# Half of the first in-projection of token blocks 2 and 3 by seven block products for eight, with the units of the second MLP made later

## The chip, the cores and the metric

The kernel runs on one core of a Trainium2 chip. The metric is the device time of one execution in microseconds (us); three runs of the kernel before gave 1089.79, 1090.01 and 1091.31 us, and their median, 1090.01 us, is the time before. A profiled execution is one more run, with its own time. PE is TensorE, DVE is VectorE, ACT is ScalarE, POOL is GpSimd, and SP is the engine whose queue issues nearly all DMAs.

## What is computed

A retention layer (linear attention with a decay per head) is followed by two MLPs, all in float32, for 4 x 768 = 3072 tokens with 8 heads of 64 (so 512 features):

```python
state = gamma[None, :, None, None] * state + np.einsum('bhd,bhe->bhde', k[:, :, t], v[:, :, t])
y[:, :, t] = scale * np.einsum('bhd,bhde->bhe', q[:, :, t], state)
...
h = np.maximum(x @ w_in, 0.0)
x = h * h @ w_out
...
xn = x / rms * rms_g
g = xn @ w_gate
out = (g * (1.0 / (1.0 + np.exp(-g)))) * (xn @ w_val) @ w_out
```

`w_in` is 512 x 2048, `w_out` 2048 x 512; `w_gate` and `w_val` are 512 x 1536, and the second `w_out` 1536 x 512.

## The kernel before

**Arithmetic.** Every large product keeps float32 accuracy with a matmul type of fewer mantissa bits: an operand is split into a high and a low part (`split`, L99: an ACT copy to the high part, then a DVE subtraction, `low`, L96), and one product is three matmuls, high by high, high by low and low by high (`mm3`, L243; `proj`, L279). Weights come as 64-bit integers and are turned to float32 on the chip by a "tick" (L221): an ACT activation over the raw tile, two DVE instructions (L208, L209), then the split.

**Token blocks.** The tokens are six blocks of 512. The order of the program is written out by hand (`manual_schedule`), and each engine runs its instructions in that order.

1. Block 0, then block 1 (`block1`, L1139): for each of 16 column chunks f of `w_in`, 12 matmuls of the in-projection (`proj`), ReLU and square (`act1`), the split of the result s, and one chunk later 12 matmuls of the out-projection (`tail1`, `out1`). During block 0 the first MLP's weights are converted, two ticks a chunk.
2. Blocks 2 and 3 together: `in_phase` (L416) runs 16 chunks f times 2 blocks t, each 12 matmuls over the resident weights `W["i", f]`, into PSUM banks `ph`, with ReLU and square by ACT.
3. The out-projection of blocks 2 and 3, and everything of blocks 4 and 5 and of the second MLP, goes by Strassen's scheme: 7 products of half-size blocks for 8. A weight operand of such a product is a "unit" (512 KB: high and low part), stored in DRAM and read through a ring of seven SBUF tiles, one unit for each product of 12 matmuls. `in_pair` (L767) makes four chunks of `w_in` for two token blocks from 7 products P1, P2, P6, P5, P7, P3, P4; `pair` (L712) does the same for the second MLP.
4. The second MLP runs for s = 0, 1, 2 (two token blocks each): six `pair`s, then the out-projection. For s = 0 its weight units are made in the same pairs (`make_unit`, L670).

**Making units.** `made_units` (L143) makes four of the seven units (P5, P7, P6, P3) of a quarter q of a weight matrix in five steps, from two "rows" tiles that hold the quarter in float32: step 1 is two DVE adds or subtractions of 128x512, step 2 a split (P5), steps 3 and 4 a subtraction and a split each (P7, P6), step 5 a split (P3). The other three units (P1, P2, P4) are stored directly from the split weights (`keep_units`, L138; `keep_in`, L1228). For the first MLP the rows tiles are summed again from the split weights by four DVE adds a quarter (`whole_rows`, L1185), so a quarter takes seven steps. The out-weights' steps (`made`) are taken two a chunk in block 1, the in-weights' (`made_in`) one a chunk from f = 4 of block 1 on and then in `in_phase`, quarter order 0, 1, 2, 3. The units of the second MLP's out-weights (`makers`) are made in `in_phase`, from rows tiles that stay in SBUF from their ticks on. Those ticks begin in block 1 at chunk MORE_AT + 1 = 13.

**Retention.** The tokens come in 24 chunks of 128; chunks 8 to 15 are "visited" (`visit`, L974) in block 1 at even f, chunks 16 to 23 in `in_phase` at odd f. A visit is some 64 small matmuls through the banks `pr`, whose scores land in another bank and are masked by DVE (`mask`, L905, six instructions). `after_visit` (L983) copies the result out of `pr` (a split for blocks 2 and 3, a plain ACT copy for blocks 4 and 5), adds to the state on DVE, and issues the loads for two chunks on. POOL multiplies state, v and q by their decays (L959, L881, L870).

**Storage.** 38 SBUF tiles of 4 KB a partition serve weights, operands, ring, rows and raw loads alike; a new tile waits for the last use of the one whose place it takes. `stores()` issues the DMAs put off in `later`.

**Where order binds** (the program's order of DVE around the end of block 1):

```python
if f in visit_at:
    after_visit(at_chunk, sink(at_chunk), kv)
...
last_of(f)
tail1()
prev = (f, s, j)
```

`last_of` (here `last1`, L1254) holds `made`, the tick and `made_in`; `tail1` is the out-projection of the chunk before. The low part of s of chunk f therefore stands in DVE's queue behind all that `last1` of chunk f - 1 put there.

## Time and profile before

| | |
|---|---|
| median of three runs | 1090.01 us |
| profiled execution: its own time | 1091.34 us |
| its span, first to last instruction | 1089.6 us |
| PE busy | 1084.2 us, 6305 matmuls |
| DVE busy | 793.4 us, 1109 instructions |
| ACT busy | 565.9 us, 877 instructions |
| POOL busy | 74.9 us, 65 instructions |
| DMA | 277.79 MB, mean 255 GB/s |
| granted TensorE clock, mean | 0.999 |

The span is what the engines show; 1.7 us of the profiled time lie around it. Shares of busy time are averages over stages that differ: what an edit costs is read from the stage that it is in. A matmul's duration in the rows (0.39 us) is its way through the array; the pace at which they follow one another is the difference of their starts.

Stages in the trace, by the starts of PE's groups: block 0 until 117 us, block 1 from 117.5 to 229.5, `in_phase` from 229.5 to 341.3, the out-projection of blocks 2 and 3 to 417.7, `in_pair`s of blocks 4 and 5 to 494, their out-projection to 570.9, then the second MLP, whose six pairs of s = 0 run from 570.87 to 685.

### The profile page before, as it was taken

How to read it: one execution, taken by the hardware profiler on the slowest of the kernel's cores; microseconds unless marked ns; L12 is line 12 of the kernel's file. 1: busy time of each engine (PE TensorE's matmuls, PEld its weight loads, DVE VectorE, ACT ScalarE, POOL GpSimd, SP SyncE). 2: the span in 40 equal slices, each digit the busy share in tenths (PEclk: the TensorE clock that was granted, in tenths of full speed). 3: DMA queues.
4: the chain of work that ended last, by engine and by line, in shares of the span. 5: the costliest groups of instructions: out<-in, count | busy, mean ns of one | idle time of the engine just before them, and what ended most of it. 6: DMA issues, size and time to landing. Idle time of an engine off the chain costs nothing.

```text
span 1089.6 us, 16607 instructions
## 1 busy us (share of the span) xinstructions
PE 1084.2 (100%) x6305; PEld 893.1 (82%) x6305; DVE 793.4 (73%) x1109; ACT 565.9 (52%) x877; POOL 74.9 (7%) x65
## 2 busy tenths in 40 slices
PE   9999999999999999999999999999999999999998
PEld 7788888887888888888888888888888888888887
DVE  6988689989976996578887676995333896433585
ACT  5777434467767546785455555453332554233442
POOL 3000142214210000000000000000000000000000
PEclk9999999999999999999999999999999999999999
DMA  9964678898999669985646769667667567666563
GB/s 362 356 213 148 217 247 301 300 364 297 347 379 350 219 231 398 367 293 193 212 174 250 270 242 350 221 211 250 194 232 251 193 213 249 193 193 194 193 212 117
DMA packets 100963, 277.79 MB, mean 255 GB/s; under 512 B 10212, under 2 KB 33532, under 8 KB 100884
## 3 DMA queue, kind: packets, MB, share of 16 engines
q1 hardware_dynamic: 100704, 276.49, 72.7%
q8 instruction: 50, 0.82, 0.3%
q10 hardware_dynamic: 180, 0.24, 0.1%
q14 instruction: 29, 0.24, 0.1%
HBM read 195.41 MB, written 81.28 MB: 254 GB/s over the span
## 4 chain that ended last, share of the span: by engine, by line
PE 97%; DMA 1%; DVE 1%; ACT 0%; issue 0%; ACTq 0%; SPq 0%
PE ph L286 14%; PE ph L244 9%; PE ph L246 9%; PE ph L245 9%; PE pa L244 8%; PE pa L246 8%; PE pa L245 8%; PE pb L244 5%; PE pb L246 5%; PE pb L245 5%; PE pr L244 3%; PE pr L246 3%; PE pr L245 3%; PE pr L939 2%; PE pr L948 1%; PE pr L928 1%
## 5 line engine op out<-in xcount | busy, mean ns | idle before, releaser
L286 PE MATMUL ph<-xh,w_i 128*128 128x512 f32 x504 | 162.6, 392 | 0.1
L467 ACT CAST o<-act 128x1024 fp32r<-128x1024 f32 x101 | 105.6, 1052 | 109.4 <-DVE act L104 50.6
L97 DVE TENSOR_TENSOR o<-act,o 128x1024 fp32r<-128x1024 f32 x101 | 122.9, 1219 | 29.1 <-ACT o L467 29.0
L286 PEld LDWEIGHTS ph<-xh,w_i 128*128 128x128 f32 x504 | 94.5, 188 | 21.1 <-ACT act L426 0.5
L286 PE MATMUL ph<-xl,w_i 128*128 128x512 f32 x252 | 97.6, 389 | 0.0
L245 PE MATMUL ph<-o,ring 128*128 128x512 f32 x228 | 88.6, 389 | 0.0
L246 PE MATMUL ph<-o,ring 128*128 128x512 f32 x228 | 88.5, 388 | 0.0
L244 PE MATMUL ph<-o,ring 128*128 128x512 f32 x228 | 88.5, 388 | 0.0
L244 PE MATMUL ph<-xop,ring 128*128 128x512 f32 x176 | 68.6, 390 | 0.0
L245 PE MATMUL ph<-xop,ring 128*128 128x512 f32 x176 | 68.5, 389 | 0.0
L246 PE MATMUL ph<-xop,ring 128*128 128x512 f32 x176 | 68.5, 389 | 0.0
L244 PE MATMUL pa<-xop,ring 128*128 128x512 f32 x176 | 68.5, 389 | 0.0
L245 PE MATMUL pa<-xop,ring 128*128 128x512 f32 x176 | 68.5, 389 | 0.0
L246 PE MATMUL pa<-xop,ring 128*128 128x512 f32 x176 | 68.5, 389 | 0.0
L245 PE MATMUL pb<-xop,ring 128*128 128x512 f32 x176 | 68.5, 389 | 0.0
L244 PE MATMUL pb<-xop,ring 128*128 128x512 f32 x176 | 68.5, 389 | 0.0
L246 PE MATMUL pb<-xop,ring 128*128 128x512 f32 x176 | 68.5, 389 | 0.0
L107 DVE TENSOR_TENSOR part<-pr,part 128x512 f32<-128x512 f32 x38 | 25.9, 689 | 55.7 <-ACT part L111 54.4
L104 DVE TENSOR_TENSOR act<-act 128x1024 f32<-128x1024 f32 x52 | 63.4, 1219 | 0.3
L111 ACT COPY part<-ph 128x512 f32<-128x512 f32 x52 | 30.3, 587 | 58.6 <-PE ph L246 58.4
L706 ACT ACTIVATE t<-part 128x512 f32<-128x512 f32 x54 | 34.1, 632 | 46.8 <-DVE part L107 46.8
L286 PEld LDWEIGHTS ph<-xl,w_i 128*128 128x128 f32 x252 | 47.3, 188 | 9.5
(249 smaller groups left out, 2520.3 us busy)
## 6 DMA issues: line engine op xcount, KB each, us to landing
ring<-wu SPq DMA_DIRECT2D x84, 512.0 KB, 4.2
ring<-up SPq DMA_DIRECT2D x63, 512.0 KB, 4.3
ring<-uo SPq DMA_DIRECT2D x56, 512.0 KB, 4.1
wu<-ring SPq DMA_DIRECT2D x42, 512.0 KB, 5.5
ring<-ui SPq DMA_DIRECT2D x28, 512.0 KB, 5.2
raw<-w1i SPq DMA_DIRECT2D x16, 512.0 KB, 9.2
raw<-w1o SPq DMA_DIRECT2D x16, 512.0 KB, 8.7
vkt<-vk SPq DMA_DIRECT2D x16, 512.0 KB, 5.6
```

Source lines behind the costliest of these rows:

```text
L97: eng.tensor_tensor(out=dst_l, in0=src, in1=dst_h.bitcast(F32), op=ALU.subtract)
L104: eng.tensor_tensor(out=out_, in0=a, in1=b, op=ALU.subtract)
L107: eng.tensor_tensor(out=out_, in0=a, in1=b, op=ALU.add)
L111: nc.scalar.copy(dst[:, m], acc[m])
L244: nc.tensor.matmul(acc, ah, bh, start=start, stop=False, **more)
L245: nc.tensor.matmul(acc, ah, bl, start=False, stop=False, **more)
L246: nc.tensor.matmul(acc, al, bh, start=False, stop=stop, **more)
L286: nc.tensor.matmul(h, w[:, a, k * 128:(k + 1) * 128], x[b][k], start=n == 0, stop=n == len(order) - 1)
L467: nc.scalar.copy(h, src)
L706: nc.scalar.activation(t, g, AF.Silu)
L928: nc.tensor.matmul(kv[b, p, :], kk[:, p, h, :], vv[:, p, h, :], start=True, stop=True)
L939: nc.tensor.matmul(a[heads[h ^ SWAP[p]], :], vv[:, p, h, :], P[:, h, p, :], start=(p == 0 or two and p == 2), stop=(c < B and p in (1, 3)) ...
```

## The change

`in_phase` keeps chunks 0 to 7 only (NCL = 4 pairs of chunks). Chunks 8 to 15 are made by two `in_pair`s, n = 2 and 3, ahead of the out-projection. For that

- blocks 2 and 3 leave the visits of block 1 as plain copies (`Raw`), and a new generator, `first_x`, makes the operands P1 and P2 (block 2) at f = 10 and 12 of block 1, `other` and P3 (block 3) at f = 14, and the rest in the eight chunks of `in_phase`;
- float32 rows of the chunks 8 to 15 of both first-MLP weights are stored to DRAM (`kept`) when they are converted in block 0; `whole_rows` loads them back for quarters 2 and 3 in place of its DVE adds, so those quarters take six steps; the in-weights' quarters are made in the order 2, 3, 0, 1;
- visits 20 to 23, eight ticks and the last unit steps move into the two pairs (`after1b`); ticks begin at f = 10 of block 1 (MORE_AT = 9);
- the seven ring tiles are loaded at f = 1 to 7 of `in_phase`, first with in-units of quarters 2 and 3;
- the rows of the second MLP's out-weights go to DRAM (`rows2`), and `made_late` loads them and makes those units in the first pairs of s = 0: one step before `act2` of P1 (`first`), two after P6 (`second`), one after P3 (`third`).

```diff
@@ -39,13 +39,14 @@
-MORE_AT = 12
+MORE_AT = 9
-RING_AT = 12
+NCL = 4
+RING_AT = 16
...
+    rows2 = [[dram.tile([128, 2, 512], F32, name=f"rows_p{q}{r}") for r in range(2)] for q in range(NQ2)]
+    kept = {(k, n): dram.tile([128, 2, 512], F32, name=f"rows_{k}{n}") for k in "io" for n in range(NCL, 2 * NQ)}
...
@@ -126,9 +129,11 @@
         t = slot(f"w_{key[0]}{key[1]}", F32R)
         W[key] = t
         nc.scalar.copy(t[:, 0, :], f)
+        if key[1] >= 2 * NCL:
+            nc.sync.dma_start(kept[key[0], key[1] // 2][:, key[1] % 2, :], f)
         return lambda: low(eng or nc.vector, t[:, 1, :], f, t[:, 0, :])
...
-    def make_some():
-        if makers and next(makers[0], makers) is makers:
-            makers.pop(0)
+    def made_late():
+        for q in range(NQ2):
+            rows = [slot("rows") for _ in range(2)]
+            for to, kept_rows in zip(rows, rows2[q]):
+                nc.sync.dma_start(to, kept_rows)
+            yield
+            yield from made_units(uo2, q, rows, lambda: slot("sm")[:, 0, :])
 
             if n % 4 == 3:
-                makers.append(made_units(uo2, n // 4, row_tiles.pop(n // 4), lambda: slot("sm")[:, 0, :]))
+                for to, rows in zip(rows2[n // 4], row_tiles.pop(n // 4)):
+                    later.append(lambda to=to, rows=rows: nc.sync.dma_start(to, rows))
...
     def magnitude(i):
         if i < upto[0] and i not in sizes:
             key = steps[i][1]
-            sizes[i] = row_of(key[1]) if key[0] == "p" else cf.tile([128, 512], F32, tag="f", name="f")
+            if key[0] == "p":
+                sizes[i] = row_of(key[1])
+            elif key[0] in "io" and key[1] >= 2 * NCL and i % 3 == 0:
+                sizes[i] = tp.tile([128, TB], F32, tag="y", name="f")
+            else:
+                sizes[i] = cf.tile([128, 512], F32, tag="f", name="f")
...
     def in_phase(xs, w_of, after, between):
-        for f in range(NF1):
+        for f in range(2 * NCL):
...
+    def first_x(raws, xs):
+        y = {(h, t): raws[t].t[:, 2 * h:2 * h + 2, :] for h in range(2) for t in range(2)}
+
+        def put(src, wide=False):
+            if wide:
+                t = big("xop", F32R)
+                o = [t[:, 0:2], t[:, 2:4]]
+            else:
+                o = [slot("xop", F32R) for _ in range(2)]
+            split(*o, src, nc.vector)
+            return o
+
+        yield
+        X[P1] = put(y[0, 0])
+        yield
+        X[P2] = put(y[1, 0])
+        yield
+        other = put(y[0, 1])
+        X[P3] = put(y[1, 1])
+        for a in ((X[P1], X[P2]), (other, X[P3])):
+            xs.append([[a[k // 2][n][:, k % 2, :] for k in range(KC)] for n in range(2)])
+        yield
+        sub(y[0, 0], y[0, 1], y[0, 0])
+        yield
+        X[P5] = put(y[0, 0])
+        yield
+        sub(y[0, 1], y[1, 1], y[0, 1])
+        yield
+        X[P7] = put(y[0, 1], True)
+        yield
+        sub(y[1, 1], y[1, 1], y[0, 0])
+        yield
+        X[P6] = put(y[1, 1])
+        yield
+        sub(y[1, 0], y[1, 0], y[1, 1])
+        yield
+        X[P4] = put(y[1, 0], True)
         yield
...
             rows = row_tiles[key, q] = [slot("rows") for _ in range(2)]
+            if 2 * q >= NCL:
+                for r in range(2):
+                    nc.sync.dma_start(rows[r], kept[key, 2 * q + r])
+                yield
+                return
...
         def in_units():
-            for q in range(NQ):
+            for q in (2, 3, 0, 1):
...
         def sink1(c):
+            nonlocal coming_xs
             t = c // B - 2
-            if t == len(xs):
-                xs.append(Operand(t == 0))
-            return xs[t]
+            if t == len(raws1):
+                raws1.append(Raw())
+                if t:
+                    coming_xs = first_x(raws1, xs)
+                    next(coming_xs)
+            return raws1[t]
...
+        def more_ring():
+            n = len(ring)
+            ring.append(slot(f"ring{n}", F32R))
+            nc.sync.dma_start(ring[n].bitcast(F32), stream[n])
+
+        stream += [ui[q][k] for q in range(NCL // 2, NQ) for k in IN_ORDER]
         def last1(f):
             stores()
+            if f >= RING_AT:
+                more_ring()
             if f == MORE_AT:
                 more_steps(W2_SOON)
@@ -1260,6 +1333,8 @@
                 tick()
             if f >= 4:
                 next(made_in, None)
+            if f in (10, 12, 14):
+                next(coming_xs)
...
+        def next_chunk():
+            nonlocal at_chunk
+            decay_v(at_chunk + 1, nc.gpsimd)
+            decay_q(at_chunk + 2, nc.gpsimd)
+            at_chunk += 1
+
         def after1(f, t):
-            nonlocal at_chunk
             if t == 0:
                 stores()
                 tick(ahead=f < 8)
                 if f and f % 2 == 0:
-                    decay_v(at_chunk + 1, nc.gpsimd)
-                    decay_q(at_chunk + 2, nc.gpsimd)
-                    at_chunk += 1
-            elif f in (10, 12, 14):
-                tick(ahead=False)
+                    next_chunk()
             elif f % 2:
                 kv, _ = visit(at_chunk, pa, True)
                 after_visit(at_chunk, sink2(at_chunk), kv)
-            if t or f not in (2, 4, 6, 8):
-                make_some()
+            if t:
+                next(coming_xs, None)
             if f % 2 == 0 or t == 0:
                 next(made_in, None)
-            if f >= RING_AT and t:
+            if t and f and len(ring) < 7:
                 more_ring()
-            if (f, t) in ((14, 1), (15, 0), (15, 1)):
-                n = (f - 14) * 2 + t - 1
-                out_1.hi(n)
-                out_1.lo(n)
-
-        def more_ring():
-            n = len(ring)
-            ring.append(slot(f"ring{n}", F32R))
-            nc.sync.dma_start(ring[n].bitcast(F32), stream[n])
+
+        def after1b(n, k):
+            background()
+            mask()
+            stores()
+            if k in (P1, P5, P7, P4):
+                tick(ahead=False)
+            if (n, k) == (NCL // 2, P1) or k == P5 or k == P4 and n < NQ - 1:
+                next_chunk()
+            if k in (P6, P3):
+                kv, _ = visit(at_chunk, (ph, pb)[(n + 1) % 2] if k == P6 else pa, True)
+                after_visit(at_chunk, sink2(at_chunk), kv)
+            if k in (P1, P5, P7, P4):
+                next(made_in, None)
+            if n == NQ - 1 and k in (P2, P6, P3):
+                i = (P2, P6, P3).index(k)
+                out_1.hi(i)
+                out_1.lo(i)
 
         in_phase(xs, lambda f: W[("i", f)], after1, between1)
-        while len(ring) < 7:
-            more_ring()
+        for _ in coming_xs:
+            pass
+        for n in range(NCL // 2, NQ):
+            in_pair(n, after1b)
+        for a in last_square:
+            square_of(a)
+        last_square.clear()
         while back:
             if due:
                 sums(pa[0])
             background()
 
-        while makers:
-            make_some()
         for _ in made_in:
             pass
         stores()
...
+                def make_late(n):
+                    for _ in range(n if s == 0 else 0):
+                        next(making, None)
+
                 def first():
+                    make_late(1)
...
                 def second():
                     nonlocal coming
+                    make_late(2)
...
                 def third():
+                    make_late(1)
```

## Rows read from the trace of the kernel before

**Rows 1.** The page: busy time by engine; the chain that ended last, by engine.

```profile
PE 1084.2 (100%) x6305; PEld 893.1 (82%) x6305; DVE 793.4 (73%) x1109; ACT 565.9 (52%) x877; POOL 74.9 (7%) x65
...
PE 97%; DMA 1%; DVE 1%; ACT 0%; issue 0%; ACTq 0%; SPq 0%
```

**Rows 2.** Windows: length, busy PE, PEld, DVE, ACT, POOL; clock, DMA share, GB/s.

```profile
20.00:33.00 13.00, 12.88 (x95) 9.51 (x93) 11.71 (x21) 10.44 (x19) 2.97 (x2) 1.00 1.03 405
...
180.00:229.50 49.50, 49.37 (x419) 40.55 (x418) 48.04 (x83) 25.29 (x47) 15.82 (x12) 1.00 0.87 313
229.50:341.30 111.80, 111.70 (x949) 91.22 (x947) 91.83 (x161) 76.32 (x137) 24.87 (x20) 1.00 0.94 341
...
608.95:627.99 19.04, 19.04 (x86) 15.77 (x85) 13.74 (x21) 9.44 (x17) 0.00 (x0) 1.00 0.64 234
```

**Rows 3.** Chain in order of time, PE, start of in_phase: start, length, what.

```profile
235.09 8.16 PE ph L286 x36
```

**Rows 4.** Timeline of DVE, end of block 1: start, length, instruction, [idle before, releaser].

```profile
193.58 0.42 DVE L911 TENSOR_TENSOR causal<-ph,seen_sb 128x256 f32<-128x256 f32 x1 [0.76 <-PE ph L893]
...
195.49 0.69 DVE L97 TENSOR_TENSOR s<-r,s 128x512 fp32r<-128x512 f32 x1
...
198.84 3.24 DVE L107 TENSOR_TENSOR rows<-w_o 128x512 f32<-128x512 f32 x2
...
202.87 1.22 DVE L107 TENSOR_TENSOR rows<-w_o 128x512 f32<-128x512 f32 x2
...
212.22 2.55 DVE L107 TENSOR_TENSOR rows<-w_i 128x512 f32<-128x512 f32 x2
...
224.41 0.75 DVE L97 TENSOR_TENSOR xl<-pr,xh 128x256 fp32r<-128x256 f32 x2
...
229.92 0.68 DVE L97 TENSOR_TENSOR s<-r,s 128x512 fp32r<-128x512 f32 x1
```

**Rows 5.** Timeline of POOL, after a visit of block 1.

```profile
198.34 1.49 POOL L881 TENSOR_TENSOR vkt<-vkt,vdec_sb 128x512 f32<-128x512 f32 x1
199.78 1.74 POOL L870 TENSOR_TENSOR qnt<-qnt,qdec_sb 128x512 f32<-128x512 f32 x1
```

**Rows 6.** Timeline of PE: second out-projection matmul of block 1's last chunk.

```profile
232.44 0.39 PE L245 MATMUL pa<-s,w_o 128*128 128x512 f32 x1
```

**Rows 7.** Timeline of DVE in in_phase: two ticks; the mask after visit 19.

```profile
236.74 0.69 DVE L97 TENSOR_TENSOR wps<-rows,wps 128x512 fp32r<-128x512 f32 x1 [0.92 <-ACT wps L100]
...
242.37 0.69 DVE L97 TENSOR_TENSOR wps<-rows,wps 128x512 fp32r<-128x512 f32 x1 [1.90 <-ACT wps L100]
242.98 0.42 DVE L208 TENSOR_SCALAR rows<-rows 128x512 int32<-128x512 int32 x1
243.44 0.69 DVE L209 SCALAR_TENSOR_TENSOR rows<-raw,rows 128x512 int32<-128x512 int32 x1
...
292.64 0.42 DVE L911 TENSOR_TENSOR causal<-pa,seen_sb 128x256 f32<-128x256 f32 x1
```

**Rows 8.** Timeline of PE: the scores of visit 19.

```profile
287.71 0.85 PE L893 MATMUL pa<-qnt,kTt 64*64 64x128 f32 x32
```

**Rows 9.** Timeline of DVE, third and fourth pair of s = 0.

```profile
622.62 1.75 DVE L343 RECIPROCAL rr<-rr 128x256 f32<-128x256 f32 x1
624.28 1.22 DVE L107 TENSOR_TENSOR part<-ph,part 128x512 f32<-128x512 f32 x2
...
642.91 1.28 DVE L107 TENSOR_TENSOR part<-pb,part 128x512 f32<-128x512 f32 x2
```

**Rows 10.** Timeline of PE: where P4 starts in those two pairs.

```profile
626.11 0.39 PE L244 MATMUL ph<-xop,ring 128*128 128x512 f32 x1
...
645.15 0.39 PE L244 MATMUL pb<-xop,ring 128*128 128x512 f32 x1
```

**Rows 11.** DMA issues of 180:229.5 and 229.5:285.7: KB each, median us to landing.

```profile
raw<-w2o SPq DMA_DIRECT2D x5, 512.0 KB, 8.4
...
qnt<-qT SPq DMA_DIRECT2D x3, 256.0 KB, 5.8
```

More of the change, by code (lines that the diff above doesn't have):

```diff
@@ L128, in finish1 @@
         nc.scalar.copy(t[:, 0, :], f)
+        if key[1] >= 2 * NCL:
+            nc.sync.dma_start(kept[key[0], key[1] // 2][:, key[1] % 2, :], f)
         return lambda: low(eng or nc.vector, t[:, 1, :], f, t[:, 0, :])
-    row_tiles, makers = {}, []
+    row_tiles = {}
     def row_of(n):
@@ L1186, in whole_rows @@
             rows = row_tiles[key, q] = [slot("rows") for _ in range(2)]
+            if 2 * q >= NCL:
+                for r in range(2):
+                    nc.sync.dma_start(rows[r], kept[key, 2 * q + r])
+                yield
+                return
             for r in range(2):
@@ L1232, in keep_in @@
                 nc.sync.dma_start(units(ui[q][k])[:, m], w[:, :, h * HALF:(h + 1) * HALF])
-        xs = []
+        xs, raws1 = [], []
         made_in = in_units()
+        coming_xs = None
         def sink1(c):
+            nonlocal coming_xs
             t = c // B - 2
-            if t == len(xs):
-                xs.append(Operand(t == 0))
-            return xs[t]
+            if t == len(raws1):
[4 more added lines that the diff above has]
+            return raws1[t]
         def early1(f):
@@ L1484, in retention_then_two_mlps @@
         pairs3 = {}
+        making = made_late()
         def pair3(n):
```

## The prediction, made before the changed kernel ran

> **What bounds the kernel now.** I read the page's busy times and its chain first. PE is busy 1084.2 of 1089.6 us, and 97% of the chain that ended last is PE [rows 1]; the 5.4 us it is idle lie, but for some tenths, at the start and the end of the span. So time is won only by giving PE less to do, and lost wherever PE is made to wait. Next I read the stages: in the second half of block 1 DVE is busy 48.04 of 49.5 us and the DMA engines 0.87 of the time; in `in_phase` it is 91.83 of 111.8 and 0.94 [rows 2]. Both are stages that the change loads anew, with little room. Then I read DVE's timeline where its work has a due time.
>
> The profiled execution took 1091.34 us, 1.7 more than its span and 1.33 more than the median of 1090.01. All terms below are differences, so I apply them to the median. A difference under 0.2%, 2.2 us, can't be told from none.
>
> **What PE is spared.** Chunks 8 to 15 for two blocks are 8 x 2 x 12 = 192 matmuls. Two pairs of 7 products of 12 are 168. In `in_phase` 36 matmuls take 8.16 us [rows 3], 0.2267 us each; in a pair, P4 of one pair to P4 of the next, 84 matmuls take 645.15 - 626.11 = 19.04 us [rows 10], again 0.2267. The 24 that go are worth **5.44 us**, all on the path. The visits stay eight, with the same small matmuls.
>
> **Block 0.** Sixteen stores of 256 KB (4.2 MB) join SP's queue. They hold each float32 tile until the store has landed; the two tiles that every third tick takes in their stead make six, and a tile is wanted again only some five ticks (13 us) after it was filled. Cover: those tiles. Without it ACT's next tick would wait out a landing, 6 to 8 us [rows 11]. I take 0, and 1 as the upper end.
>
> **The end of block 1.** Between the mask of visit 10 (193.58, where DVE had just waited 0.76 us) and the split of the last chunk's s (229.92 + 0.68 = 230.60) DVE is never idle: 37.0 us of work. PE wants that low part at its second out-projection matmul, 232.44 [rows 4, 6]. The slack is 1.8 us.
>
> Removed from this stretch: the adds of out-weight rows, 3.24 + 1.22 = 4.5 us, the adds of in-weight rows, four, 2.55 + 1.3 = 3.8; six splits out of `pr` at three visits, 0.7 a visit [rows 4], 2.0; two unit splits, 1.2. Together 11.5. Added: three ticks sooner, 3 conversions of 0.42 + 0.69 (1.06 when queued) [rows 7] and 3 splits of 0.6, 5.0; `first_x`, four 128x1024 splits, each the elements of two 512 instructions, 1.2 [rows 4], 4.7; two in-unit steps of two instructions, 2.4. Together 12.1. By this DVE ends 0.6 us later and the slack covers it.
>
> But the eight adds removed took 8.3 us where eight at 0.61 are 4.9: the rest, 3.4 us, they lost while POOL ran its decays (two adds took 3.24 us at 198.84, under the POOL rows from 198.34 to 201.5) [rows 4, 5]. POOL still runs, and now the ticks and the `first_x` splits stand in its way. The Trainium skill, "SBUF — State Buffer", section "Who interferes with whom", says that a DVE instruction with two SBUF inputs is blocked by a GpSimd instruction that reads SBUF, and that one with a single SBUF input is not. The trace agrees as far as it shows: the two splits out of PSUM took 0.75 us [rows 4]. It speaks against this change, which puts splits with two SBUF inputs for those out of `pr`.
>
> With the 3.4 us kept, DVE is 4.0 us later, and PE waits 4.0 - 1.8 = 2.2. Against this, the first tick (f = 10) waits for a raw load issued a chunk earlier, 8.4 us to landing [rows 11], so DVE idles just where POOL runs after visit 10, and a third of the loss falls on nothing. Bounds 0 and 4 (2.2 and as much again if the rows for quarter 3, loaded at f = 10 and wanted at f = 11, land late); I take **0.6**, nearer to the sum without POOL, because that sum holds no doubtful row and one of the three overlaps is free.
>
> **`in_phase`, eight chunks.** `first_x` adds four subtractions and four splits of 1.2: 9.3 us of DVE. About six of the second MLP's units are no longer made here, two instructions each: 7.3 us less. Net 2 us more; in-unit steps and ticks are as many per chunk as before. In the kernel before DVE trails here: scores of visit 19 end at 288.56, their mask starts at 292.64, 4.1 us behind [rows 7, 8], and nothing minds, since PE meets DVE only once a visit. Now PE does: after visit 19 comes pair 2, whose add of P2 out of `pr` must be done when visit 20 writes `pr`, 3 products or 8.16 us later. In DVE's queue before it stand the state (0.4), P4's split (1.2), a mask (1.9, from 193.58 to 195.49 [rows 4]), a tick (1.1) and a unit step (1.2): 5.8, and the add 1.2 (1.28 in [rows 9]). With no trail it is done in time; with 4.1 + 2 it is 4.9 late. But DVE has idle time early in `in_phase` (0.92 and 1.90 us before two splits [rows 7], and some tenths) that this work fills, so I count a trail of 2.3, not 6: done at 9.3 against 8.2, about a microsecond, less the tenths in which the visit's first matmuls run. Bounds 0 and 4; I take **0.8**. After that DVE catches up: by the same rows each of the two pairs asks some 15 us of it in 25.
>
> q and k for a visit are loaded at the visit before, now only 3 products away. Landing takes 5.8 [rows 11] and POOL's two decays about 2.5; the scores come some 2 us into the visit, at 10.3. Covered by 2 us: 0, upper end 1. The ring gets one unit per product as in other pairs, and fills seven deep before; its transfers have room, since the units of the second MLP are no longer stored here. SP has no queue of waits added but the ring's.
>
> **Pairs of s = 0.** P4 adds to the bank that P7 leaves in `main`, so it waits for DVE's add of P5. Two steps of `made_late` are put right ahead of that add. A quarter takes a load and steps 1 to 5, four of these six a pair (one, two, one): load; 1, 2; 3 in the first pair, then 4; 5, load; 1, then 2; 3, 4; 5, then load; 1, 2; 3. So behind P6 the third pair has steps 3 and 4 (two subtractions, two splits: 2.4 us), and the fourth steps 1 and 2 (an add, a subtraction, a split: 1.8, and 0.1 for ACT's copy between). In the third pair the reciprocal stands there as well: the add's first half ends at 624.28 + 0.61 = 624.89 and P4 starts at 626.11 [rows 9, 10]. Slack 1.2: PE waits **1.2**. In the fourth, 643.52 against 645.15, slack 1.6: PE waits **0.3**. The first pair has the fourth's steps with less of the norm beside them, the second only a split: 0. Bounds: 1.2 if the estimate for the fourth is high, and 3.5 if its rows, two loads issued some 6 us before they are wanted, land 2 us late. I take 1.5. Elsewhere in those pairs DVE, busy 13.74 us of 19.04 [rows 2], has room for the 3.7 it is given. On SP a quarter brings two loads and four stores of 512 KB ahead of `make_unit`'s loads; DVE's sum of two quarters waits for these, but behind the add of P5, and the unit it leads to is wanted a product or two later: 0, and in the 3.5.
>
> **Sum.** -5.44 + 0.6 + 0.8 + 1.5 = -2.5: 1087.5 us by the median; a profiled execution like that of before would take 1088.8.
>
> **Rivals.**
>
> *All hidden* (0.18). Block 1's waits and pair 2's stay in the slack, and only the third pair's is paid: -5.44 + 1.2 leaves 1085.8, or 1084.6 with none; middle 1085.2. For it: the sums without POOL's share and without a trail. Against: [rows 9, 10] leave no room there.
>
> *DVE's backlog is passed on* (slower, 0.18). From f = 10 of block 1 to pair 2 DVE has no idle time left; each us that the loads or POOL cost it reaches PE, at the last chunk's s and at the add before visit 20. At the upper ends 4 + 2.5 + 1.5 = 8.0: 1092.6. It decides once DVE ends block 1 over 5 us later than before. For it: 48.04 of 49.5 [rows 2]. Against: PE's own waits give DVE time back.
>
> *The DMA queue is the bound* (no change, 0.22). The second half of block 1 moves 313 GB/s x 49.5 us = 15.5 MB. Four loads of rows (2.1), four more raw loads (2.1), early out-units (1.3), stored rows (1.05) and a unit (0.5) make 22.5 MB. At the 405 GB/s of the fullest stretch [rows 2] that takes 55.6 us, 6 too many; loads that DVE waits for land later, and 2.5 of the gain go: 1090.0. For it: the sum. Against: most of these transfers are wanted three ticks later, and `in_phase` has 6% free. The Trainium skill, "DMA: Bandwidth & Descriptors", opening table, gives a limit of about 358 GB/s for a core's HBM traffic; by it 22.5 MB would be an estimated 63 us. The 405 GB/s that the trace shows, SBUF to HBM and back, differ from it, and the measurement decides.
>
> *The change does not do what it says* (0.02): as many matmuls as before, 1090.
>
> **How the numbers follow.** My forecast has 0.40, with a range of its own of 1086 to 1089.2; three tenths of it lie beyond 2.2 us of gain, one tenth within. Faster: 0.29 + 0.18 = 0.47. No change: 0.11 + 0.22 + 0.02 = 0.35. Slower: 0.18. The range takes in the middle of "all hidden" and most of the slower case: 1084.8 to 1092.0.
>
> **What would show it.** PE's count falls by 24 128x512 matmuls. In block 1 the split of the last chunk's s ends later than PE's second out-projection matmul could start, by 0 to 1 us. In the third pair of s = 0 PE waits for DVE `part` ahead of P4, 1.2 us, and for nothing in the first two. Visit 20 waits for DVE's add in `pr`, under 2 us. I am wrong in size if block 1 alone costs over 2 us, wrong in kind if PE waits for DMA or ACT.

## The result: 1.2% slower, and the profile after

The changed kernel takes 1103.62 us (median of 4 runs, 1102.86 to 1104.49); the kernel before, on the same chip, 1090.05. The ratio is 1.0122, 95% interval 1.0105 to 1.014: 13.6 us slower, where 2.5 less was forecast.

The page of the changed kernel (busy times; the chain that ended last, by engine), its span 1102.4 us:

```profile
PE 1083.9 (98%) x6281; PEld 890.5 (81%) x6281; DVE 793.6 (72%) x1103; ACT 573.5 (52%) x880; POOL 77.1 (7%) x65
...
PE 82%; DMA 7%; DVE 6%; ACT 2%; issue 1%; SPq 1%; POOL 0%; DVEq 0%; POOLq 0%; ACTq 0%
```

The 24 matmuls are gone (x6281 for x6305 in [rows 1]), yet PE is busy 0.3 us less, not 5.4, and idle 1102.4 - 1083.9 = 18.5 us, for 5.4 before. So the 12.8 us by which the span grew are 13.1 of new waiting and 5.1 of matmuls that ran slower, less 5.4 saved. The chain, 97% PE before, has 18% of other things in it, DMA first. The same stages as in [rows 2]:

```profile
180.00:229.50 49.50, 44.80 (x386) 36.65 (x385) 38.40 (x66) 28.17 (x49) 11.67 (x9) 0.93 0.98 360
229.50:341.30 111.80, 110.34 (x942) 89.85 (x941) 90.02 (x153) 72.61 (x121) 31.81 (x23) 1.00 1.00 370
```

In block 1's second half DVE is busy 38.40 us, ten less than before: it does not lack time, it waits. The DMA share rose from 0.87 and 0.94 to 0.98 and 1.00. What PE waited for from 195 to 715 us (engine, line, what it waited for: us in total, times, longest):

```profile
PE ph L947 <- issue: 4.7, 1, 4.7
PE pb L259 <- DVE part L110: 4.0, 1, 4.0
PE pb L259 <- ACT part L114: 1.2, 2, 0.8
PE pa L260 <- DVE s L100: 0.7, 1, 0.7
PE pa L947 <- POOL qnt L924: 0.7, 1, 0.7
PE ph L259 <- DVE part L110: 0.6, 1, 0.6
PE ph L259 <- ACT part L114: 0.5, 1, 0.5
```

They add up to 12.4 us. The rest is mostly a wait of 0.9 us for q and k at the start of block 0, which comes and goes between the runs below (none with three steps a pair).

**The 4.7 us** lie at f = 12 of block 1, and behind them stands one load. SyncE's queue issues the rows of out-weight quarter 3 behind three raw loads, q, k and v of a visit and stores of units; DVE, ACT, PE and the chain of waits of the same stretch follow, one view each:

```profile
195.38 2.45 SPq L1243 DMA_DIRECT2D rows<-rows_o  x2
```
```profile
197.04 1.23 DVE L100 TENSOR_TENSOR xop<-raw,xop 128x1024 fp32r<-128x1024 f32 x1 [0.82 <-ACT xop L103]
205.88 0.69 DVE L110 TENSOR_TENSOR sm<-rows 128x512 f32<-128x512 f32 x1 [7.62 <-DMA rows<-rows_o]
...
208.63 0.68 DVE L100 TENSOR_TENSOR s<-r,s 128x512 fp32r<-128x512 f32 x1
```
```profile
206.61 0.62 ACT L103 CAST made<-sm 128x512 fp32r<-128x512 f32 x1 [7.25 <-DVE sm L110]
...
208.95 0.57 ACT L314 ACTIVATE r<-ph 128x512 f32<-128x512 f32 x1
```
```profile
209.62 1.56 PE L947 MATMUL ph<-qnt,kTt 64*64 64x128 f32 x32 [4.70 <-issue]
211.11 0.79 PE L259 MATMUL pa<-s,w_o 128*128 128x512 f32 x1
211.71 0.63 PE L260 MATMUL pa<-s,w_o 128*128 128x512 f32 x1
...
216.19 0.40 PE L301 MATMUL ph<-xh,w_i 128*128 128x512 f32 x1
```
```profile
197.52 8.18 DMA rows<-rows_o
```

The second load runs from 197.52 to 205.70. DVE, done at 198.3, runs its instructions in order and waits 7.62 us for it. ACT waits for DVE's sum, to cast it, and behind that cast stands the relu that reads `ph`. The scores write `ph`, so PE waits too; the profile calls that "issue", but they start 0.1 us after the relu's read ends (208.95 + 0.57). Afterwards 12 matmuls start in 216.19 - 211.11 = 5.08 us, 0.42 each for the 0.2267 of before, and the scores take 1.56 for the 0.85 of [rows 8]: 3.1 us more. The granted clock there (length, busy PE, clock, DMA share, GB/s):

```profile
205.00:210.00 5.00, 0.38 (x8) 0.91 0.80 318
210.00:215.00 5.00, 5.00 (x41) 0.50 1.01 302
215.00:220.00 5.00, 5.00 (x21) 0.91 1.05 404
```

0.50 is the lower of the two levels, 1.2 GHz. The place costs 4.7 + 3.1 = 7.8 us.

Such a wait of DVE need not cost PE anything. The rows of quarter 2, issued at 166.88, held DVE too, and PE shows no wait there: DVE had made the s of a chunk just before (at 171.31), and the next one was made at 180.04, in time.

```profile
175.61 0.69 DVE L110 TENSOR_TENSOR sm<-rows 128x512 f32<-128x512 f32 x1 [3.62 <-DMA rows<-rows_o]
```

**The 4.0 us** are the same thing in the fourth pair of s = 0, in the views of SyncE's queue, DVE and PE:

```profile
641.54 1.94 SPq L177 DMA_DIRECT2D rows<-rows_p  x2
```
```profile
650.25 0.69 DVE L110 TENSOR_TENSOR sm<-rows 128x512 f32<-128x512 f32 x1 [3.37 <-DMA rows<-rows_p]
...
653.49 1.28 DVE L110 TENSOR_TENSOR part<-pb,part 128x512 f32<-128x512 f32 x2
```
```profile
654.23 0.79 PE L259 MATMUL pb<-xop,ring 128*128 128x512 f32 x1 [4.00 <-DVE part L110]
...
659.51 0.47 PE L259 MATMUL pr<-xop,ring 128*128 128x512 f32 x1
```

The rows take 8.7 us from issue; the add of P5 stands behind their sum, P4 behind the add, and again 12 matmuls take 5.28 us for 2.72 (granted clock 0.53 from 655 to 660 us). The place costs 4.0 + 2.6 = 6.6 us.

### The profile page after: what moved, and what is told of

It is laid out like the page before. It is cut to its first block, busy times and chain, and to the rows that moved or that the text cites. A ratio compares the mean times of both kernels' runs of the same rounds, so it can differ in the third digit from the quotient of the medians.

```text
span 1102.4 us, 16685 instructions
## 1 busy us (share of the span) xinstructions
PE 1083.9 (98%) x6281; PEld 890.5 (81%) x6281; DVE 793.6 (72%) x1103; ACT 573.5 (52%) x880; POOL 77.1 (7%) x65
## 4 chain that ended last, share of the span: by engine, by line
PE 82%; DMA 7%; DVE 6%; ACT 2%; issue 1%; SPq 1%; POOL 0%; DVEq 0%; POOLq 0%; ACTq 0%
PE ph L301 9%; PE ph L259 9%; PE ph L260 9%; PE ph L261 9%; PE pa L259 7%; PE pa L261 7%; PE pa L260 7%; PE pb L259 4%; PE pb L261 4%; PE pb L260 4%; PE pr L259 3%; PE pr L261 3%; PE pr L260 3%; DMA rows<-rows_p 1%; DMA ui<-made 1%
## 5 line engine op out<-in xcount | busy, mean ns | idle before, releaser
L259 PE MATMUL pb<-xop,ring 128*128 128x512 f32 x192 | 76.3, 397 | 5.2 <-DVE part L110 4.0
L301 PE MATMUL ph<-xh,w_i 128*128 128x512 f32 x248 | 81.1, 390 | 0.0
L259 PE MATMUL ph<-xop,ring 128*128 128x512 f32 x192 | 75.3, 392 | 1.1 <-DVE part L110 0.6
L261 PE MATMUL pb<-xop,ring 128*128 128x512 f32 x192 | 75.7, 394 | 0.0
L260 PE MATMUL pb<-xop,ring 128*128 128x512 f32 x192 | 75.7, 394 | 0.0
L259 PE MATMUL pa<-xop,ring 128*128 128x512 f32 x192 | 74.9, 390 | 0.0
L260 PE MATMUL ph<-xop,ring 128*128 128x512 f32 x192 | 74.8, 389 | 0.0
L261 PE MATMUL ph<-xop,ring 128*128 128x512 f32 x192 | 74.7, 389 | 0.0
L261 PE MATMUL pa<-xop,ring 128*128 128x512 f32 x192 | 74.7, 389 | 0.0
L260 PE MATMUL pa<-xop,ring 128*128 128x512 f32 x192 | 74.7, 389 | 0.0
L107 DVE TENSOR_TENSOR act<-act 128x1024 f32<-128x1024 f32 x60 | 73.1, 1219 | 0.3
L301 PEld LDWEIGHTS ph<-xh,w_i 128*128 128x128 f32 x248 | 46.5, 188 | 10.3 <-ACT w_o L131 0.4
L260 PEld LDWEIGHTS ph<-o,ring 128*128 128x128 f32 x228 | 42.8, 188 | 9.3 <-DVE o L100 0.4
L259 PEld LDWEIGHTS ph<-o,ring 128*128 128x128 f32 x228 | 42.8, 188 | 8.9
```

The source lines that it names most:

```text
L107: eng.tensor_tensor(out=out_, in0=a, in1=b, op=ALU.subtract)
L259: nc.tensor.matmul(acc, ah, bh, start=start, stop=False, **more)
L260: nc.tensor.matmul(acc, ah, bl, start=False, stop=False, **more)
L261: nc.tensor.matmul(acc, al, bh, start=False, stop=stop, **more)
L301: nc.tensor.matmul(h, w[:, a, k * 128:(k + 1) * 128], x[b][k], start=n == 0, stop=n == len(order) - 1)
```

## The experiments

Theory: the float32 rows, loaded just before they are wanted, hold DVE, which holds ACT and PE; each of the two waits above was followed by matmuls at the lower clock. Rivals: the DMA volume as such is the bound ("volume"), and DVE has too much to do ("backlog"). Each ratio is to the kernel before on the same chip (1090.3 to 1090.8); microseconds "off" are counted from the changed kernel's 1103.6, which comes from a chip where the kernel before took 1090.05.

### Out-weights' rows earlier

```diff
+            if (key, q) in row_tiles:
+                return
...
+            for i, _ in enumerate(made_units(uo, q, row_tiles.pop(("o", q)), lambda: spare)):
+                if i == O_AHEAD and 2 * (q + 1) >= NCL and q + 1 < NQ:
+                    load_rows("o", q + 1)
+                yield
```

`O_AHEAD` is 1, and `load_rows` issues the two loads.

> The rows of the out-weights' quarters 2 and 3 are still brought by DMA, but issued four steps (two or three out-units' visits) earlier. Theory 'late rows': as with the adds, 1096.5 (1095.5 to 1097.5). Rival 'volume': the queue runs at a share of 0.98 to 1.05 from 170 to 250 us, so what is moved ahead makes something else late: 1101 to 1104. Rival 'DVE's backlog': no change, 1103.6.

1095.88 us, ratio 1.0052 (1.0037 to 1.0067): 7.7 off, as the theory said. The same bytes move, the DMA share from 200 to 215 us is 1.04, and DVE waits for no rows in block 1 any more. From 195 to 345 us PE's waits are now:

```profile
PE ph L302 <- DVE causal L971: 1.3, 1, 1.3
PE pa L948 <- POOL qnt L925: 0.3, 1, 0.3
```

So what cost 7.7 us was the short lead of the load, not the volume. Whether the same load on another queue would have landed in time wasn't tried.

### The second MLP's rows earlier

```diff
+        load_rows(0)
+        yield
         for q in range(NQ2):
...
+            for i, _ in enumerate(made_units(uo2, q, coming_rows.pop(q), lambda: sm)):
+                if i == P_AHEAD and q + 1 < NQ2:
+                    load_rows(q + 1)
+                yield
```

`P_AHEAD` is 1.

> The stored rows of the second MLP's out-weights are loaded four steps (about one pair) earlier, nothing else. Theory 'late rows': the 4.0 us wait in the fourth pair and the 12 matmuls at the lower clock behind it go (2.4 us): 6.4 us off, 1097.2 (1096.2 to 1098.2); the third pair's waits stay. Rival 'volume': the queue is full there too, another transfer (a quarter of the weights, the lines) is late in its place: 1101 to 1104. Rival 'DVE's order': the add of P5 is late because of the steps ahead of it, not of the load: 1103.6.

1100.55, ratio 1.0092 (1.0075 to 1.0109): 3.1 off, half of what was expected. The wait for rows is gone and the granted clock in the pairs is 1.00, but PE is still idle 3.8 us in the pairs, mostly for ACT's copies into parts, and in the profiled execution PE waited 1.7 us more between 200 and 345 us.

### Both earlier

The two edits above together.

> Both kinds of rows loaded earlier (out-weights' rows and the second MLP's), nothing else changed. If the two cures act in different stages they add: 7.7 and 3.1 us off 1103.6, 1092.8 (1091.8 to 1093.8), with 3 to 4 us of PE's idle time left in the pairs of s=0, put down to ACT's copies of P5 and P6 into parts and DVE's adds into them. If late rows were all that the change costs, 1085 to 1088. Rival 'volume': what one loads early makes the other late, 1095 to 1097.

1092.19 (10 runs), ratio 1.0015 (1.0005 to 1.0024). The cures add (7.7 + 3.1 = 10.8): 11.4 of the 13.6 us are back. The page of this kernel, span 1089.9:

```profile
PE 1079.1 (99%) x6281; PEld 886.7 (81%) x6281; DVE 793.2 (73%) x1103; ACT 574.1 (53%) x880; POOL 75.9 (7%) x65
```

PE is now busy 5.1 us less than in [rows 1], the 24 matmuls; and idle 10.8 us, 5.4 more than before, which eats them. 3.5 of these lie in the pairs of s = 0; 1.6 more than before lie between 200 and 345 us, 0.8 behind DVE's mask and 0.8 behind POOL's decay of q.

### Out-weights' rows by DVE's adds again

```diff
-            if 2 * q >= NCL:
+            if key == "i" and 2 * q >= NCL:
```

> Out-weights' quarters 2 and 3 added on DVE again, as before the change (8 more adds of about 0.91 us), and their rows neither stored nor loaded; the in-weights' rows still go by DRAM. Theory 'late rows' (a load of rows that DVE waits for at f=11 holds DVE, then ACT, then PE's scores of f=12): the 4.70 us wait goes, and with it the 12 matmuls after it at 0.43 for 0.23 us (2.4 us): 7.1 us off, 1096.5 (1095.5 to 1097.5). Rival 'volume' (the DMA queue as a whole sets the time there): 4.2 MB less at 0.37 MB per us, up to 11 us off, 1092.5. Rival 'DVE's backlog': 7.3 us more work on DVE in block 1, so 1103.6 or more.

1101.07, ratio 1.0096 (1.0081 to 1.0111): 2.5 off, a miss. The wait for `rows_o` is gone, but with the eight adds back DVE trails, waits 1.06 us for the in-weights' rows, loses 2.2 us more in three instructions that run beside POOL's decays (4.0 us for 1.8, from 214 us on), and one visit later ACT waits for it and PE's scores for ACT (ACT's and PE's timelines):

```profile
220.38 0.62 ACT L103 CAST made<-sm 128x512 fp32r<-128x512 f32 x1 [3.98 <-DVE sm L107]
```
```profile
224.40 0.90 PE L947 MATMUL ph<-qnt,kTt 64*64 64x128 f32 x32 [2.43 <-issue]
```

Late rows or late sums, the path is the same: the cast of `made` in ACT's order. The backlog is a second way into it, not a rival.

### Casts of these out-units by DVE

```diff
-            split(u[:, :, 0, :], u[:, :, 1, :], src, nc.vector)
+            if el is None:
+                split(u[:, :, 0, :], u[:, :, 1, :], src, nc.vector)
+            else:
+                el.tensor_copy(u[:, :, 0, :], src)
+                low(nc.vector, u[:, :, 1, :], src, u[:, :, 0, :])
```

> The changed kernel, but the high parts of the out-units of quarters 2 and 3 in block 1 are copied by DVE, not by ACT, so that ACT does not wait for DVE while DVE waits for rows; the rows come as late as before. Theory 'DVE held by late rows, ACT behind it': ACT's relu of f=12 and PE's scores are no longer held, but DVE's low part s of f=11 stands behind the same wait, and PE's out-projection of f=11 takes over the wait: 4.7 us becomes about 3.5, the clock falls all the same, 1102 (1101 to 1103.6). Rival 'ACT alone is what holds PE': the wait goes, 1096 to 1098.

1107.29, ratio 1.0156 (1.0142 to 1.0169): a miss in time, 3.7 us slower than the changed kernel, where 1.6 faster was expected. The path is the expected one. With ACT free the scores wait 0.59 us only, and the out-projection takes over the wait, for the low part s that stands behind the rows on DVE (PE's timeline):

```profile
206.48 0.90 PE L951 MATMUL ph<-qnt,kTt 64*64 64x128 f32 x32 [0.59 <-issue]
...
213.27 0.79 PE L264 MATMUL pa<-s,w_o 128*128 128x512 f32 x1 [5.47 <-DVE s L100]
```

So DVE held by rows (7.57 us, as before) is enough; ACT is only the nearer of two ways to PE.

### Steps behind the add of P5 (rows as late as ever)

```diff
         add(p5, main)
+        after_p5()
         make(n + 1, P5)
...
-                    make_late(2)
```

> In the pairs of s=0 the two middle steps of the late out-units stand behind DVE's add of P5 instead of ahead of it; the rows are loaded as late as ever. Theory 'late rows' with DVE in order: P4 needs only that add, so the third pair's 1.2 us, the fourth's 4.0 us and the 2.4 us of lower clock go: 7.6 us off, 1096.0 (1094.5 to 1097.5), though DVE still waits for the rows. Rival 'DVE's backlog': the 3.4 us that DVE waits make its next steps late, and half or more comes back: 1100 to 1103.

1104.91, ratio 1.0133 (1.0118 to 1.0148): a miss. P4 no longer waits for the add, but ACT's casts of the steps now wait for DVE behind it, and ACT's copies of `main` into parts stand behind these: PE waits 8.7 us for ACT `part` in the pairs:

```profile
PE ph L259 <- ACT part L114: 5.6, 3, 2.6
PE pb L259 <- ACT part L114: 3.1, 3, 1.3
```

### Where in a pair the steps stand, with both rows early

Four placements. Ratio intervals are in brackets. Three steps a pair in six pairs:

```diff
-                    make_late(2)
+                    make_late(1)
```

> As the kernel with both rows early, but three steps of the late out-units in each of six pairs for four in each of the first four and a half. Theory 'DVE and ACT in order': a step's two DVE operations and its ACT copy stand ahead of the add and the copy that PE waits for, so fewer a pair leave less: 1091.5 (1090 to 1092.5), the wait in pairs 1 to 4 down by half. Theory 'late rows alone': as without it, 1092.8.

1094.14 (1.0021 to 1.0042), a miss. Then one step behind P1, none in the middle, three at the end:

```diff
-                    make_late(2)
+                    make_late(0)
...
-                    make_late(1)
+                    make_late(3)
```

> As the kernel with both rows early (1092.2), but the two middle steps of each pair stand with the last one, behind DVE's add of P6 into its part, so that three steps stand there, one behind P1's and none between the copy of P6 and the add of P5. Theory 'only steps ahead of the add of P5 cost': the 3.5 us in the pairs fall under 1, 1089.5 (1088.5 to 1090.5). Rival 'no room in a pair': the steps make the next pair's add of P2 and ACT's work behind it late, and P7 waits for ACT's copy of P6: 1092 to 1095.

1098.1 (1.0061 to 1.0088), beyond theory and rival. Then two, and three, ahead of the copy of P5:

```diff
         make(n, P4)
+        in_gap()
         take(p5, pa)
```

> As the kernel with both rows early (1092.2), but the two middle steps of the late out-units stand between the making of the next-to-last unit and the copy of P5, where DVE waited 1.15 and 2.03 us a pair in the kernel before the change; first and last step stay. Theory 'a step costs PE what it delays of the copies of P5 and P6 and of the adds': of the 3.5 us of PE's idle time in the pairs half or more goes: 1090 (1089 to 1091). Rival 'DVE has no room left in a pair': the same 1092.2, the wait only moves.

> As the kernel with both rows early, but all steps of the late out-units stand in that gap, three a pair in six pairs, and none elsewhere. Theory as before: nearly all of the 3.5 us goes, 1089 (1088 to 1090), a little faster than before the change (1090.3). Rival 'no room left': three steps together are about 2.7 us of DVE in a gap of 3.2 us, so P5's and P6's copies are late by as much as they were: 1092 to 1094, as with three steps a pair spread over it.

1099.72 (1.0067 to 1.0097) and 1102.15 (1.0088 to 1.0122). Both put the sum of the first rows soon behind their load; with two steps DVE waits 2.81 us for them, with three (DVE and then PE):

```profile
580.03 0.69 DVE L112 TENSOR_TENSOR sm<-rows 128x512 f32<-128x512 f32 x1 [3.91 <-DMA rows<-rows_p]
```
```profile
583.40 0.79 PE L270 MATMUL ph<-xop,ring 128*128 128x512 f32 x1 [5.68 <-ACT part L116]
```

That is the changed kernel's fault again. So these two ran once more, beside the kernel with both rows early, with the first rows loaded ahead of the pairs:

```diff
         making = made_late()
+        next(making)
```

> As the kernel with both rows early (1092.2), with the rows of the first quarter loaded ahead of the first pair as well, so that every step of the late out-units comes one place sooner. Theory 'late rows': the first pair did not wait there, so nothing is won by the load itself; the steps fall on other places of the pairs: 1091 to 1093. If the order of steps within a pair is what the 3.5 us hang on, the waits move from pair to pair and the time stays the same.

> As the kernel with two steps ahead of the copy of P5 (1099.7), whose first pair waited 4.58 us behind rows loaded in that same pair, now with these rows loaded ahead of it. Theory 'late rows': that wait and the lower clock after it go, 7 us off, 1092.7 (1091.5 to 1093.5), and the other waits for ACT's copies (2.5 and 2.1 us) stay. Theory 'the gap is the right place, only the load was late': 1088.5 to 1090.

> The same for the kernel with three steps a pair in the gap (1102.2, its first pair's wait 5.68 us). Theory 'late rows': 5.7 us and about 2.5 of lower clock off, 1094 (1093 to 1095). Theory 'the gap is the right place': 1088.5 to 1090.

1093.38 (1.0016 to 1.0034), 1097.67 (1.0048 to 1.0075), 1095.77 (1.0037 to 1.0062). With three steps the load was worth 6.4 us for the 8.2 expected; with two, 2.1 for 7: the other waits for ACT's copies grew from 4.6 to 7.5 us, and DVE waits 1.0 us for rows again. No placement is under the 1092.2 of the one that the change has; the first of these three can't be told from it.

### Whose time is it

Casts of the late out-units by DVE (the edit as above, for these units), both rows early:

> As the kernel with both rows early, but the high part of each late out-unit is copied by DVE itself, not by ACT, so that ACT no longer waits for DVE's sums in these steps (12 copies of about 0.6 us more on DVE, 12 fewer on ACT). Theory 'ACT held by DVE': the waits of PE for ACT's parts (2 to 3 us in the pairs of s=0) go: 1090.5 (1089.5 to 1091.5). Rival 'DVE's backlog': DVE is the one that is behind, 7 us more work there: 1093 to 1097.

1095.81, ratio 1.0044 (1.0029 to 1.0059): worse, so ACT's waiting alone is not what is left. Then the sums, and the sums and low parts, by POOL:

```diff
-            split(u[:, :, 0, :], u[:, :, 1, :], src, nc.vector)
+            split(u[:, :, 0, :], u[:, :, 1, :], src, el)
...
-        plus(sm, a21, a22)
-        sub(a21, a11, a21)
+        plus(sm, a21, a22, se)
+        sub(a21, a11, a21, se)
```

`se` is POOL in both runs, `el` only in the second.

> As the kernel with both rows early (1092.2), but the four sums of each quarter of late out-units (12 in all) are made by POOL, which does nothing in these pairs; the casts stay on ACT and the low parts on DVE. If the 3.5 us left in the pairs are DVE's time, 8 us of it are taken off: 1089.5 to 1090.5. If what holds PE is ACT waiting in order for a sum, a sum on POOL (1.3 to 1.5 us in block 1's rows, for 0.69 on DVE) comes later still: 1093 to 1096.

> As the one before, with the low parts on POOL as well, so that the late out-units take nothing of DVE at all (24 operations, 16 us less on DVE; 24 of about 1.4 us on POOL). Theory 'DVE's time': all of the 3.5 us goes, 1088.5 to 1089.5, faster than before the change by 0.1 to 0.2%. Rival 'POOL stands in DVE's way' (in block 1 DVE's 0.69 us rows take 1.2 to 1.8 while POOL runs): DVE loses what it was spared, 1092 to 1095.

1094.37 (1.0023 to 1.0043) and 1094.1 (1.0021 to 1.0044). Neither helps, and DVE's time shows a reason. From 580 to 700 us (length, busy PE, PEld, DVE, ACT, POOL; clock, DMA share, GB/s), with both rows early, and with all 24 operations on POOL:

```profile
580.00:700.00 120.00, 116.50 (x508) 94.50 (x507) 101.75 (x157) 64.43 (x111) 0.00 (x0) 1.00 0.90 333
```
```profile
580.00:700.00 120.00, 115.88 (x506) 94.27 (x505) 99.95 (x133) 64.68 (x111) 33.79 (x24) 1.00 0.90 332
```

DVE has 24 instructions of 0.69 us less, 16.5 us, and its busy time falls by 1.8. The others got longer. The groups by line of the one, then of the other (count, busy us, mean ns):

```profile
L772 DVE TENSOR_TENSOR act<-part,t 128x512 f32<-128x512 f32 x17 | 11.7, 687 | 0.4 <-ACT t L771 0.2
L112 DVE TENSOR_TENSOR part<-pa,part 128x512 f32<-128x512 f32 x12 | 7.8, 684 | 0.4 <-PE pa L272 0.4
```
```profile
L773 DVE TENSOR_TENSOR act<-part,t 128x512 f32<-128x512 f32 x17 | 17.0, 1000 | 1.2 <-POOL made L102 0.6 <-ACT t L772 0.5
L112 DVE TENSOR_TENSOR part<-pa,part 128x512 f32<-128x512 f32 x12 | 7.8, 681 | 0.3 <-PE pa L273 0.3
```

Products of two SBUF tensors went from 687 to 1000 ns; adds that read one of the two from PSUM stayed. The Trainium skill, "SBUF — State Buffer", section "Who interferes with whom", says that a DVE instruction with two SBUF inputs contends with a GpSimd instruction that reads SBUF, and one with at most one such input, outside the modes that use both port pairs, does not; the trace agrees on both. So POOL's idle time in these pairs is not free for such work.

### The units back in the first in-projection

With the out-weights' rows early, the second MLP's out-units made in the first in-projection again, one step at nearly every product:

```diff
+                makers.append(made_units(uo2, n // 4, row_tiles.pop(n // 4), lambda: slot("sm")[:, 0, :]))
...
+            if t or f > 3:
+                make_some()
...
+            make_some()
```

> Out-weights' rows early, and the second MLP's out-units made in the first in-projection again, as before the change, with their rows neither stored nor loaded; the pairs of s=0 do nothing new. Theory (late rows, and steps ahead of adds in the pairs): the pairs are as before the change, their 5.9 us of idle time and about 1.5 us of lower clock go from 1095.9: 1088.5 (1087.5 to 1089.5), that is the block products' own worth. Rival 'DVE's backlog': some 26 us of DVE's work comes back into the first in-projection, whose block products leave it 5.4 us less time: 1092 to 1096.

1117.34, ratio 1.024 (1.0225 to 1.0256): far off. In the pairs of s = 0 PE has no idle time, as expected, so the 3.5 us left there come with the steps; but in the first in-projection it has 19.97 us, from 230 to 345. DVE is busy 89.3 us of these 115 and not full. PE waits for ACT's evictions into `act`, and ACT, for its casts, for stores to land:

```profile
PE ph L307 <- ACT act L447: 11.6, 6, 5.1
```
```profile
ACT made L104 <- DMA up<-wps: 10.7, 3, 3.9
```

That the units' buffers are what runs out is likely, but wasn't tried; how the block products do by themselves, with units made as before, stays open.

## Why the prediction was wrong

**PE spared, 5.44: right.** 24 matmuls, 5.1 us of busy time with both rows early.

**Block 0 at 0: right.** PE is busy 50.00 of 50 us from 50 to 100 and from 100 to 150.

**The end of block 1, 0.6: the step that failed.** PE's wait for the last chunk's s is there, 0.7 us, but that is luck: with the out-weights' rows early it is gone, and PE waits 0.8 to 1.3 us for a mask instead. The late rows stood in the prediction only as an upper end of this term ("as much again if the rows for quarter 3, loaded at f = 10 and wanted at f = 11, land late"): 2.2 us at a due time four out-units later. They were late (issued from 195.38, wanted at 198.3, there at 205.7; DVE 7.6 idle), and they cost 7.8 at once, because DVE and ACT work in order, and the relu and s of the very next chunks stand behind the sum. The landing time was on the table: 8.4 us for a raw load [rows 11], where an out-unit takes (229.92 - 195.49) / 5 = 6.9 [rows 4], on queues that were to get fuller. It was read for the raw loads, where it only filled a gap, and not put against the due time of the rows. Both alarms that the prediction named went off: block 1 cost over 2 us, and PE waited behind ACT and, through DVE, behind DMA.

The prediction's reading that the trace bears out POOL's rule on two splits out of PSUM does not hold: they ran from 224.41 to 225.16 [rows 4], and POOL began only after them (POOL's timeline before the change). What bears the rule out is the run with 24 operations on POOL.

```profile
225.64 0.93 POOL L959 TENSOR_TENSOR st<-st,sdec_sb 128x256 f32<-128x256 f32 x1 [9.72 <-DVE st L107]
```

**in_phase, 0.8: not there.** No add out of `pr` held PE. q came 0.7 us late at one visit, within the upper end of 1 given to a 0.

**Pairs of s = 0, 1.5: half right, and the second failed step.** The third pair's P4 waited 0.6 for 1.2, and its P7 0.5. The fourth's rows were the bound of 3.5 ("land 2 us late"); DVE waited 3.37, PE 4.0, and the cost was 6.6, since the granted clock fell. And DVE's "room for the 3.7 it is given" is not room: eleven runs that moved or re-assigned the steps left PE idle 3.9 to 9.0 us from 580 to 700 us, for 3.5 where the change has them once both rows are early. Busy 13.74 of 19.04 does not say how much of the rest is waiting in step with ACT, which has to copy P6 before P7 may add to the same bank; PE's waits for ACT `part` show that path, but no run takes it away alone.

**The clock: no term.** By the starts of the matmuls it took 3.1 + 2.6 us.

**The rivals.** "The DMA queue is the bound" named the event, loads that DVE waits for, and mispriced it: 2.5 us from the volume. The queue was indeed full, at a share of 0.98, but at 360 GB/s, and moved 360 x 49.5 = 17.8 MB in that stretch, not 22.5. With the volume unchanged and the loads earlier 7.7 us come back, so it was the lead of one load. "DVE's backlog is passed on" had the sign, but DVE was idle 7.6 us where it was to be full; a backlog shows only in the run with the adds back. The chance of 0.18 for slower was small because these prices were.

With both loads early the 5.4 us saved are eaten by 5.4 us of waiting, 3.5 of it in the pairs that have the steps. No version here is faster than the kernel before.

## What to carry to other kernels

Work moved from an engine to DMA is not off the path until the load's issue stands a full landing time, under the load of its new stage, ahead of its first use: put landing time against due time for every load that an in-order engine waits for, and price it by everything queued behind that wait on this engine and on those that wait for it, not by the next due time you happen to know. Count the clock in too: here PE's waits of 4.7 and 4.0 us brought another 3.1 and 2.6 us of slower matmuls. And spare busy time of an engine is room only if its gaps aren't waits in step with another engine.

## What was not expected of the hardware

The clock after short waits: after PE waited 4.70, 4.00 and, with the adds back, 2.43 us, the next matmuls started 0.42 to 0.43 us apart; with both rows early its waits were 1.2 us at most in the pairs, and the granted clock 1.00 throughout. Between these the length of the wait does not decide it: with one step behind P1 and three at the end of a pair, matmuls 0.42 us apart followed a wait of 2.58 us; with the steps behind the add of P5 a wait of 2.62 us was followed by matmuls 0.23 us apart, but for the first:

```profile
671.04 0.50 PE L259 MATMUL ph<-xop,ring 128*128 128x512 f32 x1 [2.62 <-ACT part L114]
671.38 0.40 PE L260 MATMUL ph<-xop,ring 128*128 128x512 f32 x1
671.62 0.39 PE L261 MATMUL ph<-xop,ring 128*128 128x512 f32 x1
```

What decides it stays open. And the price of POOL's help: 33.8 us of its work cost DVE 14.7 us of stretched instructions.
